# Start-up of a fused convolution and gated feed-forward kernel: decode steps, taps and softmax steps given to other engines, and another order of work

## The chip, the cores and the metric

One core of a Trainium2 chip runs the whole kernel. The metric is the device time of one execution in microseconds (us), the median of several runs. The engines are named as in the profile: PE (TensorE, with PEld for its weight loads), DVE (VectorE), ACT (ScalarE), POOL (GpSimd) and SP (the queue that issues most DMAs).

## The reference, cut to what matters

There are 4 sequences of 4160 tokens with 192 channels. Each token has its own 7 convolution weights for each of 8 heads, which go through a softmax; the result goes through a gated feed-forward part of width 1024.

```python
w = softmax(weight_gen, axis=-1)                  # per token and head, 7 taps
attn[s, h] = sum_k w[s, h, k] * x[s - 6 + k, h]   # causal, zeros ahead of the sequence
h = relu(attn @ w_in)                             # 192 -> 1024
conv = sum_k conv_w[k] * h[s - 1 + k]             # 3 taps, per channel
out = (h * sigmoid(conv)) @ w_out                 # 1024 -> 192
```

## The kernel before, in words

**Blocks.** The 16640 tokens are cut into 128 stretches of 130 tokens, one stretch to a partition. A block takes 4 tokens of every stretch, 512 in all; there are 33 blocks, called b0 to b32 here. The work of a block has these stages:

- *Softmax* (`sm_ops`, L222). Weights come in groups of 8 tokens (group 0: 4), so that group 1 serves b1 and b2, group 2 serves b3 and b4, and so on. The steps are max, subtract (`sub`, L242), exp, sum, add a small number, reciprocal, multiply (`norm`, L264). In the groups that hold a stretch's first 7 tokens, `zero` (L269) multiplies by a mask. `SMX` says for groups 0 to 3 on which engine (V is DVE, G is POOL) `sub` and `norm` run; `SMR` gives both to POOL from group 4 on.
- *Taps* (`tap`, L284, the instruction at L292). Seven products of shifted tokens and weights, each 128 x 768, into four pieces `px` and three pieces `py`. `PLAN` names the engine of each of the seven for b0, b1 and b2; later blocks have all seven on POOL.
- *Sum of the taps and transpose* (`head`, L654). In b0 to b2 (form "a") PE transposes all seven pieces and adds them up in PSUM (L327). Later blocks (form "d") add them by two accumulating DMAs issued on POOL (L315, L318) and one POOL addition (L322), and PE transposes one piece.
- *Split* (L338 on ACT, L343 on DVE) of the transposed block into a high and a low part, which PE multiplies with high and low parts of `w_in`.
- *Units* (`unit`, L708): for each of 8 slices f of the 1024 channels, five matmuls into a bank of the PSUM pool z (L359, five banks), relu (L365, ACT), the middle tap of the 3-tap convolution (L369, ACT), the two side taps (L376, DVE), tanh (L383, ACT), the gate product (L392, DVE). A z bank is free after its gate product.
- *Out tiles* (`out_tiles`, L733): 16 matmul instructions for each 128 tokens (L405), evacuation (L414, ACT), store.

**Weight decode at the start.** `w_in` comes in five pieces (`CH`; "m" rows 0 to 127, "f" the other 64 rows folded, which a DMA spreads to their place, L614), `w_out` in four (`WOE`), and `conv_w` in one. Each arrives in 64-bit floats that are decoded by integer and float steps (`dec`, L529): two on ACT (L133, L136), then clamp (L140), shift (L143), sign (L146) and add (L151). `w_in` pieces are then split into high (L595, ACT) and low (L600). The last letter of a piece's string is its mode. In mode S the bits stay in SBUF, and the first two letters name the engines of clamp and add. In mode P they are in the one bank of the PSUM pool `ps_d`, and all steps, the low part too, run on DVE whatever the letters say:

```python
mode = eng[2]
ce, je = "VV" if mode == "P" else eng[:2]
```

Pieces in mode P follow each other through `dbank`, since they share the bank; odd out tiles use it later.

**Order of the work.** All stages are tasks with an engine, an estimated duration and dependencies. A planner (L776 to L863) places them by earliest start and rank `now`, then from the end back and once more forward, keeps the shorter plan, and the instructions are issued in that order, so each engine runs a fixed list. The rank of a block's taps is its number plus `TO`, of its transposes plus `FO`, of its out tiles plus `WO_`; `FORD` is the order of the slices in b0. The engine "VK" marks a DVE task with operands in SBUF alone; the plan reserves POOL during such a task. Where a POOL task follows VK tasks in the list, L874 and L875 put a DVE memset and a POOL memset of the same small tile `tok` ahead of it, so that POOL waits until DVE has come that far:

```python
if eng[i] == "VK":
    pend = True
elif eng[i] == "G" and pend:
    t_ = tok[nk % len(tok)]
    V.memset(t_, 0.0)
    G.memset(t_, 1.0)
```

Of the kernel before, what the change touches and what calls it, by code (L numbers as in the profile page):

```python
# [17 lines left out]
TAPS = 7  # L18
# [1 line left out]
GRP = 24  # L20
G7 = "G" * 7
PLAN = (
    ("a", "GVVGGGG"),
    ("a", "GVVGGGG"),
    ("a", "GVVGGGG"),
)
REST = ("d", G7)
SMX = ("VV", "VV", "VV", "VG")
SMR = "GG"
TO = -3.05  # L30
FO = -0.65
WO_ = 1.47
NX = 3
NY = 2
NZ = 5
# [2 lines left out]
RING = 24  # L38
CG = 2
CH = (  # L40
    ("f", 0, 256, 5.2, "VVS", "V"),
    ("m", 0, 256, 8.7, "VVS", "G"),
    ("f", 256, 512, 17.0, "GGP", "G"),
    ("m", 256, 512, 16.0, "VVS", "V"),
    ("m", 512, 1024, 18.0, "VVP", "V"),
)
FORD = (1, 3, 2, 7, 0, 6, 5, 4)
SL = ((0, 1, 2), (3, 4, 5), (1, 0, 2), (4, 3, 5), (1, 4, 5))
WOE = ("VGP", "VGP", "GVS", "GVS")


def vec(n, ps=1):

    return 0.07 + n / 960 + 0.06 * ps


def act(n, ptr=0):
    return 0.05 + n / 1200 + 0.1 * ptr


def pool(n, ins=2):
    return (0.13 + n / 437) if ins == 2 else (0.1 + n / 900)
# [3 lines left out]
def kernel(  # L66
# [15 lines left out]
    HK = HEADS * TAPS  # L82
# [104 lines left out]
    def grows(j):  # L187
        return (R * (2 * j - 1), 2 * R) if j else (0, R)
# [33 lines left out]
    def sm_ops(j):  # L222
        s0, n = grows(j)
        V = nc.vector
        es = SMX[j] if j < len(SMX) else SMR
        E_ = [V if e == "V" else nc.gpsimd for e in es]
        N = n * HEADS * TAPS
        ed = [vec(N, 0) if e == "V" else pool(N) for e in es]
        ek = ["VK" if e == "V" else "G" for e in es]

        def w():
            return w_t[j][:, :n * HEADS]

        def m(k):
            return sm_t[j][k][:, :n * HEADS]

        def vmax():
            sm_t[j] = [sm_p.tile([P, 2 * R * HEADS, 1], F32, tag=t, name=t) for t in ("m", "r")]
            V.tensor_reduce(out=m(0)[:, :, 0], in_=w(), axis=AX.X, op=ALU.max)

        def sub():
            E_[0].tensor_tensor(out=w(), in0=w(), in1=m(0).to_broadcast([P, n * HEADS, TAPS]), op=ALU.subtract)  # L242

        def exp():
            nc.scalar.activation(out=w(), in_=w(), func=ACTF.Exp)

        def vsum():
            V.tensor_reduce(out=m(0)[:, :, 0], in_=w(), axis=AX.X, op=ALU.add)

        def eps():  # L250
            if j:
                nc.scalar.activation(out=m(0), in_=m(0), func=ACTF.Copy, bias=1e-9)
            else:
                V.tensor_scalar(out=m(0), in0=m(0), scalar1=1e-9, scalar2=None, op0=ALU.add)

        def rec():
            V.reciprocal(out=m(1), in_=m(0))

        def keep():
            r = m(1)[:, (n - 1) * HEADS:, :]  # L260
            V.tensor_scalar(out=r, in0=r, scalar1=mask[:, 1:2], scalar2=None, op0=ALU.mult)

        def norm():
            E_[1].tensor_tensor(out=w(), in0=w(), in1=m(1).to_broadcast([P, n * HEADS, TAPS]), op=ALU.mult)  # L264

        def zero():
            k = min(n, TAPS - s0)
            t4 = w()[:, :k * HEADS, :].rearrange("p (s h) k -> p s h k", h=HEADS)
            V.tensor_tensor(  # L269
                out=t4, in0=t4, in1=edge[:, s0:s0 + k, :].unsqueeze(2).to_broadcast([P, k, HEADS, TAPS]), op=ALU.mult  # L270
            )

        return (
            [("V", vec(N, 0), vmax), (ek[0], ed[0], sub), ("A", act(N) + 0.04, exp), ("V", vec(N, 0), vsum),
             ("A" if j else "VK", 0.16 if j else 0.1, eps), ("V", 0.07 + 0.05 * n, rec)]
            + ([("VK", 0.1, keep)] if j == NG - 1 else [])
            + [(ek[1], ed[1], norm)]
            + ([("VK", vec(N, 0), zero)] if s0 < TAPS else [])
        )

    def tap_cut(q, k):
# [140 lines left out]
    V, G = nc.vector, nc.gpsimd  # L422

    with tc.manual_schedule():
# [41 lines left out]
        def load_out(c):  # L466
            nc.sync.dma_start(
                out=r_out[c].rearrange("p (c d) b -> p c (d b)", c=2),
                in_=w_out.bitcast(I32)[2 * c * P:2 * (c + 1) * P, :].rearrange("(c p) e -> p c e", p=P),
            )  # L470
# [16 lines left out]
        def task(eng, dur, deps, fn=None, after=(), begun=()):  # L487
            edges = [(d, dur_of(d) + lat(d, eng)) for d in deps if d is not None]
            edges += [(d, dur_of(d)) for d in after if d is not None]
            edges += [(d, 0.0) for d in begun if d is not None]  # L490
            tasks.append((eng, dur, edges, fn))
            prio.append(now[0])
            return len(tasks) - 1
# [12 lines left out]
        def dma(occ, deps, fn):  # L506
            return task("none", 3.2, [task("H", occ, deps, fn)])
# [9 lines left out]
        def softmax(q, dep):  # L517
            t_ = dep
            for i, (e, d, fn) in enumerate(sm_ops(q)):
                t_ = task(e, d, [t_] + ([sm.get(q - 2)] if i == 0 else []), fn)  # L520
            sm[q] = t_
# [57 lines left out]
        def used(ix):  # L579
            return [k for i in ix for k in last_use[i]]  # L580

        for c, (kind, a, b, t, eng, wle) in enumerate(CH):
            n = b - a
# [43 lines left out]
        for c in range(4):  # L627
# [3 lines left out]
                wo[:, 2 * c:2 * c + 2].rearrange("p c d -> p (c d)").bitcast(I32), r_out[c],  # L631
                slots[iB][:, 0:w], slots[iC][:, 0:w], dma(1.6, spreads, lambda c=c: load_out(c)), used((iB, iC)), WOE[c],
            )
# [12 lines left out]
        def loads(q):  # L646
            if q >= RB:
                x_t_[q] = dma(1.2, all_taps[q - RB], lambda: load_x(R * q - 1, R * q + 3))
            g = group(q)
            if g >= WB and g not in sm:  # L650
                g0 = 2 * (g - WB)
                softmax(g, dma(0.7, all_taps[g0] + (all_taps[g0 - 1] if g0 else []), lambda: load_w(g)))

        def head(q):  # L654
# [24 lines left out]
            multi = len(out_) > 1  # L679
            now[0] = q + FO  # L680
            hold, prev = {}, [None, None]
# [26 lines left out]
        def unit(j, f):  # L708
            n = j * NF + f
            so = 1 if j else 0  # L710
            now[0] = j + (FORD.index(f) if j == 0 else f) / NF
            mm[n] = task(
# [20 lines left out]
        def out_tiles(j):  # L733
            d_ = 0.03 + NF * 0.326
            no = geom(j)[0]
            for i in range(no):
                now[0] = j + WO_ + i / R
                hold = {}
                z_ = j == NB - 1 and i % 2 == 0

                def fn(i=i, hold=hold, z_=z_):
                    hold[0] = mm2(j, i, ps_z.tile([P, W], F32, tag="z", name="z") if z_ else None)
                dep = [mm[NU - 1], (zl + zfree)[-NZ]] if z_ else bank[1 + i % 2]
                a_ = tiles[j, i] = task(
                    "P", d_, [rd[j * NF + f] for f in range(NF)] + wo_rdy + dep, fn,
                    after=[tiles.get((j, i - 1))])
                e_ = task("A", act(D) + 0.02, [a_] + (stored[-4:][:1] if i == 0 and len(stored) > 3 else []),
                          lambda hold=hold: evac(*hold[0]), begun=last_evac)
                last_evac[:] = [e_]
                if z_:  # L750
                    zfree.append(e_)
                else:
                    bank[1 + i % 2] = [e_]
                if j == NB - 1 and i % 2 == 1:
                    dma(0.5, [e_], lambda i=i: store(j, i - 1, i + 1))
            if j < NB - 1:
                stored.append(dma(1.2, [e_], lambda: store(j, 0, no)))

        def attention(q):
            now[0] = q + TO  # L760
            loads(q)
            head(q)
# [3 lines left out]
        for j in range(NB):  # L766
            if j >= 2:
                out_tiles(j - 2)
            for f in FORD if j == 0 else range(NF):
                unit(j, f)  # L770
# [137 lines left out]
```

## Time and profile before

| | us |
|---|---|
| median of 3 runs (lowest to highest) | 724.79 (724.45 to 724.89) |
| profiled execution, its own time | 722.55 |
| its span, first to last instruction | 720.8 |
| PE busy | 693.8 (96%) |
| DVE busy | 633.2 (88%) |
| ACT busy | 546.9 (76%) |
| POOL busy | 503.8 (70%) |
| mean granted TensorE clock | 0.998 |

Busy shares are averages over the span; the start has other limits than the rest, so it is read by stretches of time. A row of the timeline gives the start, the busy time, the engine, the line, the operation and, in brackets, how long the engine sat idle before it and what released it.

### The profile page before, as it was taken

What the parts mean: (1) busy time and instruction counts of PE and PEld (TensorE: products, weight loads), DVE (VectorE), ACT (ScalarE), POOL (GpSimd) and SP (SyncE); (2) the same over time, 40 slices, a digit from 0 to 9 for tenths busy, and PEclk for the clock granted to TensorE, in tenths of its full rate; (3) what the DMA queues carried; (4) which work ended last, traced back from release to release, by engine and by line L of the source; (5) the groups of instructions that cost most, each with busy time, mean ns of one, the idle gap of its engine ahead of it and who ended that gap; (6) DMA issues with size and microseconds to landing.
All of it is one profiled execution on the core that took longest, in us unless ns stands there. A gap on an engine that the chain in (4) does not pass through costs nothing.

```text
span 720.8 us, 10895 instructions
## 1 busy us (share of the span) xinstructions
PE 693.8 (96%) x3809; PEld 630.0 (87%) x3809; DVE 633.2 (88%) x981; ACT 546.9 (76%) x1049; POOL 503.8 (70%) x390
## 2 busy tenths in 40 slices
PE   2799999899999999999999999999999999999998
PEld 1678898799999999999999999999999999999998
DVE  6999997899998989989898988999888888888882
ACT  3397887787878778878787787778777777787872
POOL 3588998969888789888777687887767767810000
PEclk9999999999999999999999999999999999999999
DMA  7635999997999888888898788878887886862111
GB/s 230 174 111 119 215 216 228 208 238 167 222 204 211 195 196 190 180 194 199 199 209 196 177 188 178 197 185 202 201 189 185 187 191 133 175 150 77 69 48 45
DMA packets 70787, 127.59 MB, mean 177 GB/s; under 512 B 5046, under 2 KB 42573, under 8 KB 70732
## 3 DMA queue, kind: packets, MB, share of 16 engines
q0 software_dynamic: 20160, 58.99, 47.0%
q1 hardware_dynamic: 50090, 67.51, 28.3%
q8 instruction: 30, 0.49, 0.3%
q10 hardware_dynamic: 482, 0.40, 0.2%
q14 instruction: 25, 0.20, 0.1%
HBM read 20.51 MB, written 12.78 MB: 46 GB/s over the span
## 4 chain that ended last, share of the span: by engine, by line
PE 82%; POOL 10%; DMA 4%; issue 2%; DVE 1%; ACT 1%; SPq 0%; POOLq 0%
PE ops L405 41%; PE z L359 36%; POOL py L292 4%; POOL px L292 4%; PE tp L327 3%; DMA px<-py 2%; DMA ring<-in_x_dram 1%; POOL px L318 1%; PE z L405 1%; DMA stage<-in_moe_w_in_dram 1%; POOL px L322 0%; POOL px L315 0%; DVE px L292 0%; POOL w L242 0%; SPq L437 0%
## 5 line engine op out<-in xcount | busy, mean ns | idle before, releaser
L376 DVE SCALAR_TENSOR_TENSOR z<-h,cw,z 128x512 f32<-128x512 f32 (+1 forms) x528 | 377.6, 741 | 14.7 <-ACT z L369 10.5
L405 PE MATMUL ops<-wo,g 128*128 128x192 f32 x2048 | 353.2, 326 | 0.0
L405 PEld LDWEIGHTS ops<-wo,g 128*128 128x128 f32 x2048 | 338.8, 190 | 10.2 <-DVE H L343 0.4
L359 PE MATMUL z<-H,wi 128*128 128x512 f32 x1056 | 304.3, 410 | 3.4 <-DVE g L392 3.4
L292 POOL TENSOR_TENSOR px<-ring,w 128x768 f32<-128x768 f32 (+2 forms) x141 | 229.6, 1774 | 66.8 <-PE tp L327 66.5
L359 PEld LDWEIGHTS z<-H,wi 128*128 128x128 f32 x1056 | 191.9, 189 | 35.6 <-DVE g L392 4.4
L392 DVE SCALAR_TENSOR_TENSOR g<-z,h 128x512 f32<-128x512 f32 (+1 forms) x264 | 179.5, 681 | 34.7 <-ACT z L383 32.0
L383 ACT ACTIVATE z<-z 128x512 f32<-128x512 f32 (+1 forms) x264 | 152.1, 577 | 61.7 <-DVE z L376 60.6
L369 ACT ACTIVATE z<-h,cw 128x512 f32<-128x512 f32 (+1 forms) x264 | 180.1, 683 | 5.4
L365 ACT ACTIVATE h<-z 128x512 f32<-128x512 f32 x264 | 156.0, 592 | 34.1 <-PE z L359 33.7
L292 POOL TENSOR_TENSOR py<-ring,w 128x768 f32<-128x768 f32 (+2 forms) x109 | 167.8, 1852 | 0.0
L359 PE MATMUL z<-L,wi 128*128 128x512 f32 x264 | 103.4, 392 | 0.0
L322 POOL TENSOR_TENSOR px<-px 128x768 f32<-128x768 f32 x30 | 68.2, 2275 | 8.5 <-DMA px<-px 8.5
L318 POOL DMA_DIRECT2D px<-px x30 | 38.3, 1275 | 31.5 <-DMA px<-py 31.2
L359 PEld LDWEIGHTS z<-L,wi 128*128 128x128 f32 x264 | 49.7, 188 | 11.4
L338 ACT ACTIVATE H<-tp 128x512 fp32r<-128x512 f32 (+1 forms) x63 | 37.2, 591 | 25.5 <-PE tp L327 25.3
L327 PE MATMUL tp<-ident,px 128*128 128x128 f32 (+1 forms) x288 | 45.5, 282 | 6.6 <-POOL px L292 3.5
L414 ACT ACTIVATE o<-ops 128x192 f32<-128x192 f32 x128 | 41.8, 326 | 10.6 <-PE ops L405 10.4
L327 PEld LDWEIGHTS tp<-ident,px 128*128 128x128 f32 (+1 forms) x288 | 34.4, 133 | 15.0 <-POOL px L292 5.5
L315 POOL DMA_DIRECT2D px<-py x30 | 42.7, 1424 | 6.4 <-POOL py L292 6.3
L343 DVE TENSOR_TENSOR L<-tp,H 128x512 fp32r<-128x512 f32 x33 | 22.7, 688 | 13.5 <-ACT H L338 13.4
L343 DVE TENSOR_TENSOR H<-tp,H 64x512 fp32r<-64x512 f32 x30 | 20.5, 683 | 2.2 <-ACT H L338 1.3
(81 smaller groups left out, 187.0 us busy)
## 6 DMA issues: line engine op xcount, KB each, us to landing
px<-py POOLq DMA_DIRECT2D x30, 1152.0 KB, 10.5
h<-h SPq DMA_DIRECT2D x128, 256.0 KB, 4.9
px<-px POOLq DMA_DIRECT2D x30, 768.0 KB, 6.8
ring<-in_x_dram SPq DMA_DIRECT2D x31, 384.0 KB, 7.9
out_dram<-o SPq DMA_DIRECT2D x31, 384.0 KB, 6.9
w<-in_weight_gen_dram SPq DMA_DIRECT2D x15, 224.0 KB, 7.2
r_out<-in_moe_w_out_dram SPq DMA_DIRECT2D x4, 384.0 KB, 5.3
wi<-scr SPq DMA_DIRECT2D x8, 128.0 KB, 5.8
```

The costliest lines, as they stand in the source:

```text
L292: eng.tensor_tensor(out=dst[:, a:b, :].rearrange("p s (h g) -> p s h g", g=GRP), in0=ring[:, p:p + n, :].rearrange("p s (h g) -> p s h g", ...
L318: nc.gpsimd.dma_start(out=fl4(px_t[q][:, 0:2]), in_=fl4(px_t[q][:, 2:4]), accum_op=ALU.add, max_dma_last_dim=3072)
L322: nc.gpsimd.tensor_tensor(out=a, in0=a, in1=b, op=ALU.add)
L327: nc.tensor.matmul(dst[0:D2 if part else P, c * P:(c + 1) * P], lhsT=src[:, c, part * P:part * D2 + P], rhs=ident, is_transpose=True, star ...
L343: nc.vector.tensor_tensor(out=H[D2:P, :] if part else h_t[q, "L1"], in0=tp[r, :], in1=H[r, :].bitcast(F32), op=ALU.subtract)
L359: nc.tensor.matmul(out=z, lhsT=w[:, fs], rhs=h_t[j, nm], start=(i == 0), stop=(i == len(terms) - 1))
L365: nc.scalar.activation(out=hrow(f, 2, R), in_=z_t[j, f], func=ACTF.Relu)
L369: nc.scalar.activation(out=z_t[j, f][:, :no * P], in_=hrow(f, cc, no), func=ACTF.Copy, scale=cw[:, NF + f:NF + f + 1])
L376: nc.vector.scalar_tensor_tensor(out=z, in0=hrow(f, cc + d, no), scalar=cw[:, k * NF + f:k * NF + f + 1], in1=z, op0=ALU.mult, op1=ALU.add,)
L383: nc.scalar.activation(out=z, in_=z, func=ACTF.Tanh, scale=0.5)
L392: nc.vector.scalar_tensor_tensor(out=g_of(j, f), in0=z_t[j, f][:, :no * P], scalar=1.0, in1=hrow(f, cc, no), op0=ALU.add, op1=ALU.mult)
L405: nc.tensor.matmul(out=ps[:, 0:D], lhsT=g_of(j, f)[:, i * P:(i + 1) * P], rhs=wo[:, f, :], start=(f == 0), stop=(f == NF - 1),)
```

## The change

It gives new values to tables and to one engine argument. Taps of b1 and b2 run on POOL, all seven; in b0 the two DVE taps are numbers 1 and 4 in place of 1 and 2. `sub` and `norm` of groups 2 and 3 run on POOL. Every piece of `w_in` and `w_out` is decoded in mode P. `zero` runs on the engine of `norm` and is planned with its true size. `FORD`, `TO`, `FO` and `WO_` have new values.

```diff
 PLAN = (
-    ("a", "GVVGGGG"),
-    ("a", "GVVGGGG"),
-    ("a", "GVVGGGG"),
+    ("a", "GVGGVGG"),
+    ("a", "GGGGGGG"),
+    ("a", "GGGGGGG"),
 )
-SMX = ("VV", "VV", "VV", "VG")
+SMX = ("VV", "VV", "GG", "GG")
-TO = -3.05
-FO = -0.65
-WO_ = 1.47
+TO = -2.7
+FO = -0.35
+WO_ = 1.62
 CH = (
-    ("f", 0, 256, 5.2, "VVS", "V"),
-    ("m", 0, 256, 8.7, "VVS", "G"),
-    ("f", 256, 512, 17.0, "GGP", "G"),
-    ("m", 256, 512, 16.0, "VVS", "V"),
+    ("f", 0, 256, 5.2, "VGP", "G"),
+    ("m", 0, 256, 8.7, "VVP", "G"),
+    ("f", 256, 512, 17.0, "GVP", "V"),
+    ("m", 256, 512, 16.0, "VVP", "G"),
     ("m", 512, 1024, 18.0, "VVP", "V"),
 )
-FORD = (1, 3, 2, 7, 0, 6, 5, 4)
+FORD = (0, 3, 1, 5, 2, 4, 7, 6)
-WOE = ("VGP", "VGP", "GVS", "GVS")
+WOE = ("VVP", "VVP", "GVP", "VGP")
...
         def zero():
...
-            V.tensor_tensor(
+            E_[1].tensor_tensor(
...
-            + ([("VK", vec(N, 0), zero)] if s0 < TAPS else [])
+            + ([(ek[1], vec(min(n, TAPS - s0) * HK, 0) if ek[1] == "VK" else pool(min(n, TAPS - s0) * HK), zero)] if s0 < TAPS else [])
```

## Rows read from the trace of the kernel before

**Rows 1.** Busy time by stretch (PE, PEld, DVE, ACT, POOL; clock; DMA)
```profile
12.74:30.40 17.66, 11.33 (x61) 9.15 (x62) 16.43 (x30) 5.51 (x15) 11.47 (x13) 0.97 0.63 160
...
42.00:60.00 18.00, 16.44 (x96) 13.70 (x95) 17.30 (x37) 16.15 (x34) 12.85 (x11) 1.00 0.27 80
60.00:80.00 20.00, 19.99 (x108) 17.58 (x107) 19.61 (x31) 15.88 (x29) 19.68 (x19) 1.00 0.78 170
```
**Rows 2.** Chain that ended last, 0 to 140 us, shares by line
```profile
by line: POOL py L292 20.1%; POOL px L292 19.8%; issue 11.0%; DMA px<-py 9.6%; DMA ring<-in_x_dram 5.5%; PE z L359 5.2%; POOL px L318 4.0%; DMA stage<-in_moe_w_in_dram 3.1%; POOL px L322 2.5%; POOL px L315 2.3%; DVE px L292 2.2%; PE ops L40
```
**Rows 3.** Timeline of PE: first unit, and two late gaps
```profile
30.40 2.05 PE L359 MATMUL z<-H,wi 128*128 128x512 f32 x4
...
85.10 0.66 PE L327 MATMUL tp<-ident,px 128*128 128x128 f32 x4 [0.52 <-POOL px L322]
...
132.25 1.21 PE L359 MATMUL z<-H,wi 128*128 128x512 f32 x4 [2.25 <-DVE g L392]
```
**Rows 4.** POOL's waits for DVE: total, times, longest; then timeline
```profile
POOL tok L875 <- DVE tok L874: 24.8, 7, 9.6
...
12.68 0.10 POOL L875 MEMSET tok<- 128x1 f32 x1 [9.62 <-DVE tok L874]
...
16.93 0.10 POOL L875 MEMSET tok<- 128x1 f32 x1 [1.43 <-DVE tok L874]
...
20.79 0.10 POOL L875 MEMSET tok<- 128x1 f32 x1 [2.25 <-DVE tok L874]
```
**Rows 5.** Timeline of DVE: taps, and softmax subtract and normalise
```profile
17.64 1.71 DVE L292 TENSOR_TENSOR px<-ring,w 128x768 f32<-128x768 f32 x1
...
23.86 1.90 DVE L242 TENSOR_TENSOR w<-w,m 128x448 f32<-128x448 f32 x2
...
30.26 0.63 DVE L264 TENSOR_TENSOR w<-w,r 128x448 f32<-128x448 f32 x1
...
31.14 0.95 DVE L292 TENSOR_TENSOR px<-ring,w 128x768 f32<-128x768 f32 x1
...
54.69 1.82 DVE L292 TENSOR_TENSOR px<-ring,w 128x768 f32<-128x768 f32 x2
```
**Rows 6.** Groups of DVE by shape, 12.5 to 60 us: decode steps
```profile
L140 DVE TENSOR_SCALAR dps<-dps 128x384 f32<-128x384 f32 x2 | 1.1, 560 | 0.1
...
L143 DVE TENSOR_SCALAR scr<-wo 128x384 int32<-128x384 int32 x2 | 0.6, 350 | 0.0
...
L140 DVE TENSOR_SCALAR dps<-dps 128x256 f32<-128x256 f32 x1 | 0.4, 419 | 0.0
...
L600 DVE TENSOR_TENSOR scr<-dps,scr 128x256 fp32r<-128x256 f32 x1 | 0.4, 413 | 0.0
...
L140 DVE TENSOR_SCALAR scr<-scr 128x256 f32<-128x256 f32 x1 | 0.3, 280 | 0.0
```
**Rows 7.** Groups of POOL by shape, 12.5 to 60 us
```profile
L292 POOL TENSOR_TENSOR py<-ring,w 128x768 f32<-128x768 f32 x10 | 15.3, 1545 | 0.0
...
L600 POOL TENSOR_TENSOR wi<-scr,wi 128x256 fp32r<-128x256 f32 x1 | 1.1, 1108 | 0.0
L140 POOL TENSOR_SCALAR wo<-wo 128x384 f32<-128x384 f32 x2 | 1.0, 504 | 0.0
L264 POOL TENSOR_TENSOR w<-w,r 128x448 f32<-128x448 f32 x1 | 1.0, 968 | 0.0
```
**Rows 8.** Timeline: first and last steps of pieces in the decode bank
```profile
17.70 0.38 ACT L133 ACTIVATE dps<-stage 128x256 f32<-128x256 f32 x1
...
25.69 0.41 DVE L600 TENSOR_TENSOR scr<-dps,scr 128x256 fp32r<-128x256 f32 x1
...
45.53 0.51 ACT L133 ACTIVATE dps<-r_out 128x384 f32<-128x384 f32 x1
...
48.53 0.55 DVE L151 CUSTOM_DVE_ANT_0 wo<-dps,scr 128x768 uint16<-128x768 uint16 x1
...
56.43 0.55 DVE L151 CUSTOM_DVE_ANT_0 wo<-wo,scr 128x768 uint16<-128x768 uint16 x1
```

## The prediction

> **What bounds the kernel now.** The page gives PE 96% of the span, so only the rest can be won. The table by stretches says where it lies: from 60 us on PE is busy for 19.99 of 20 us, while DVE is already near its limit there (19.61). Before that PE is the engine that waits: 11.33 busy of 17.66 us between 12.74 and 30.40, 16.44 of 18.00 between 42 and 60. In the same two stretches DVE is busy for 16.43 and 17.30 us, so DVE is what is full at the start [rows 1]. The chain of waits up to 140 us names POOL first: its taps (L292) hold 40% [rows 2]. Yet POOL is busy for only 11.47 and 12.85 us of those stretches [rows 1]. The list of waits resolves this: POOL sits idle for 24.8 us in 7 waits for the token that DVE sets. The first, 9.62 us, ends at 12.68 and covers the arrival of data; 15.2 us are left [rows 4]. So POOL is late because it queues behind a full DVE, and PE is late because of both. Two late gaps of PE, 0.52 us at 85.10 and 2.25 us at 132.25 [rows 3], come from the same backlog: the first waits for POOL's sum directly, the second for a gate product. Everything after is dense PE work that the change leaves alone. A microsecond of earlier start of the dense stretch is a microsecond of time.
>
> **The change part by part.**
>
> *DVE loses work.* Two taps of b1 and two of b2: 0.95 each for b1's (the second is as long as the row at 31.14), 1.82 for b2's pair, 3.72 in all. Subtract of groups 2 and 3: 1.90. One normalise: 0.63 (the other was on POOL) [rows 5]. Together 6.25 us.
>
> *DVE gains work.* A clamp of 256 in the PSUM bank takes 0.42 us, in SBUF 0.28, and I take the shift as the same pair; three pieces of 256 go from mode S to P (the second "f" piece and the piece of 512 were in P before): 3 x 2 x 0.14 = 0.84. The low part of the second piece comes from POOL: 0.41. Two clamps of `w_out` come from POOL: 2 x 0.56. Their shifts go from 0.35 to about 0.56: 2 x 0.21 = 0.42 [rows 6]. Sign and add, which have two tensor operands, I leave at their lengths; the low part, also of two operands, is at 0.41 with one of them in PSUM [rows 6]. Together 2.8 us. Net, DVE is relieved of 6.25 - 2.8 = 3.45 us, all of it ahead of 57 us, where it is full; none is hidden.
>
> *DVE and POOL in each other's way.* The tap at 17.64, beside a POOL tap, took 1.71 us, the one at 31.14, with POOL idle, 0.95 [rows 5]. The work left on DVE that can meet this is b0's two taps and group 1's softmax, as before. I count no gain here; at best the 0.76 of one such tap, at worst the same lost.
>
> *POOL.* It gains four taps at 1.545 (6.2 us), two subtracts and one normalise at 0.97 (2.9), and loses the low part (1.11) and two clamps (1.01): net +7.0 us [rows 7]. No DMA moves with them, but the DMAs that POOL issues for b3 stand behind them in its list. Against that stand its waits. With the decode in PSUM and groups 2 and 3 on POOL, no "VK" task is left on DVE after group 1's softmax and b0's taps, both done near 20 us. So the first two waits after the start (1.43 and 2.25) stay, and the four later ones, 24.8 - 9.62 - 1.43 - 2.25 = 11.5 us, go [rows 4]. Net POOL reaches the taps of b3 4.5 us earlier. What is late next on POOL is then its own work, not DVE.
>
> *The decode bank.* Now seven pieces follow each other through one bank from about 17.7 us on. The two ends of a hold are 8.4 us (ACT at 17.70 to DVE's low part, 25.69 + 0.41) and 3.55 us (45.53 to 48.53 + 0.55) [rows 8]. Seven holds are 25 to 59 us. The long one was long because DVE was full of other work inside it; with less of that I take 5 us, 35 in all, and the last `w_out` piece is decoded near 53, against 56.43 + 0.55 = 56.98 before [rows 8]. The list behind it on DVE is b1's gate products; on SP the loads of `w_out` stand behind the spread of the second "f" piece, which leaves earlier if anything.
>
> *Numbers without a price.* `zero` stays on DVE, since groups 0 and 1 keep "VV"; only its planned length shrinks. The letters ahead of P do nothing. `FORD` starts b0 with the slice whose pieces come first, and the ranks only sort ties of a plan that is then redone; the cover is that PE has b1's transposes to fill with. If that cover is gone, the price is of the size of a gap seen late, 2.25 us [rows 3], either way.
>
> **The sum.** The dense stretch starts earlier by the smaller of two reliefs, DVE's 3.45 and POOL's 4.5: -3.45 us. Of the two late gaps (2.77 together) [rows 3] both depend on POOL's lag; POOL gains about one microsecond on PE, so I take half: -1.4. That is -4.9 us: the profiled execution would go from 722.55 (span 720.8) to 717.7. The median of the runs lies 2.24 above that execution, so it goes from 724.79 to **719.9 us**.
>
> **Rivals.**
>
> *A larger gain.* The 1.25 us between DVE's and POOL's relief, both late gaps and a slowed tap come on top: 4.5 + 2.77 + 0.76 = 8.0, and if the first unit at 30.40 also gains the 2 us that b0's taps lose to tokens and the low part, about 10: 715 to 717. For it: PE is idle for 6 of the 17.66 us ahead of the first unit [rows 1]. Against: DVE must take part in all of it, and is full. Chance 0.13.
>
> *The bank decides (slower).* If a hold takes 7 us on the mean, the last piece is ready at 17.7 + 49 = 66.7, 9.7 later than before. b1's gate products wait, its five z banks stay full and PE stops. With DVE's relief of 3.45 spent inside, that is +6.2: 731. It decides above (56.98 - 17.7)/7 = 5.6 us a hold. For it: one hold was 8.4. Against: that piece waited for DVE, not the bank. Chance 0.07.
>
> *POOL becomes the bound (slower).* If the waits for DVE stay, because a DVE task in SBUF is still put among b1's taps, POOL carries 7.0 us more, and b3's sum, which PE already waits for at 85.10 [rows 3], comes that much later: 731.8. It decides when more than 8.2 of the 15.2 us of waits stay [rows 4]. For it: a tap takes 1.545 on POOL against 0.95 on DVE [rows 5, 7]. Against: no such DVE task is left for b1 to b3. Chance 0.10.
> The Trainium skill (GPSIMD Engine Reference, Engine selection) speaks for this rival: it gives elementwise work of two inputs to VectorE, as GpSimd is about two times slower. By its measured ratio of 1.96 a tap would be an estimated 1.86 us on POOL, and the four moved ones 7.4 us in place of 6.2. The trace differs: its ratio is 1.6 [rows 5, 7].
>
> *Nothing moves.* The gain at the start is given back in a new gap of PE or ACT, for instance where ACT, in order, waits for a subtract that now runs on POOL: two gaps like that at 132.25 cost 4.5 us [rows 3] and leave 724.4. Chance 0.12.
>
> **Chances and range.** The forecast, with -2 to -7, has 0.58. A difference of 0.2%, 1.45 us, is about what the measurement tells from none. Faster: 0.58 + 0.13 and a little of the unpriced order = 0.72; same 0.11; slower 0.17. The range goes from 715.0 (the larger gain at most in full) to 725.5 (the gain given back and a little more); it leaves out the two slower rivals and the extreme of the larger gain.
>
> **What would show it.** Right: the waits of POOL for the token after 21 us are gone; the four DVE taps after 30 us are gone; the first unit begins before 29 us; the last decode of `w_out` ends before 55 us; b3's first accumulating DMA is issued some 4 us earlier; PE is dense from about 52 to 56 us on. Wrong: a hold of the bank above 5.6 us, a PE gap at b3's transpose longer than 0.52 us, ACT waiting for POOL's subtract before 60 us, or new gaps in PE after 60 us that add up to more than the old 2.77.

## The result and the profile after

The kernel after takes **714.72 us** (median of 4 runs, 713.11 to 715.78), the kernel before beside it 724.84 (724.45 to 725.26): a ratio of 0.9858 (95% interval 0.9839 to 0.9878), 10.1 us less. The sign was right and the size twice the forecast, just outside the range. The profiled execution took 713.11, its span is 711.4 (before 720.8). Executions of one kernel differ with their mean granted clock (the kernel before has a median near 722.9 over its recorded executions at 0.998 and near 724.8 over those at 0.991), and both traces are of the faster kind, 0.998 before and 1.000 after, so spans are compared with spans here and medians with medians.

**Where the time went.** Busy time by hundreds of microseconds (columns as in [rows 1]), the kernel before:

```profile
0.00:100.00 100.00, 78.44 (x437) 67.56 (x437) 89.34 (x173) 65.66 (x134) 73.77 (x73) 0.98 0.67 171
100.00:200.00 100.00, 97.68 (x535) 88.62 (x534) 89.52 (x137) 78.40 (x151) 87.60 (x67) 1.00 0.95 216
200.00:300.00 100.00, 100.00 (x550) 91.39 (x548) 91.39 (x139) 80.61 (x155) 84.03 (x62) 1.00 0.86 196
```

and the kernel after, with the stretches of [rows 1] behind them:

```profile
0.00:100.00 100.00, 81.89 (x471) 72.21 (x472) 91.06 (x176) 70.01 (x144) 82.53 (x75) 1.00 0.74 190
100.00:200.00 100.00, 100.00 (x550) 91.40 (x549) 92.19 (x141) 81.30 (x157) 93.63 (x71) 1.00 0.95 216
200.00:300.00 100.00, 100.00 (x549) 91.31 (x548) 91.17 (x138) 80.42 (x155) 81.59 (x60) 1.00 0.83 190
...
12.74:30.40 17.66, 12.31 (x69) 10.29 (x70) 16.08 (x33) 6.35 (x16) 13.80 (x14) 1.00 0.73 201
...
42.00:60.00 18.00, 17.99 (x108) 15.11 (x108) 17.91 (x35) 15.99 (x32) 17.68 (x14) 1.00 0.28 75
60.00:80.00 20.00, 20.00 (x110) 18.34 (x109) 19.61 (x31) 16.87 (x33) 17.51 (x17) 1.00 0.97 213
```

A dense stretch runs some 550 matmuls in 100 us. After, PE does 34 more in the first hundred (6.2 us at that rate) and 15 more in the second; 49 at 5.5 a us are 8.9 us, nearly all of the span's 9.4. From 200 us on the kernels are alike within a few matmuls in 100 us. The first hundred gains more PE work (6.2 us) than busy time (81.89 - 78.44 = 3.45): before, part of it ran at a granted clock of 0.50, the 1.2 GHz level, from 29.60 to 32.60, after PE's waits for b0, which is worth some 1.5 us of that difference; after shows 1.00. Over the whole span PE idles 5.7 us less (27.0 to 21.3) and is busy 3.7 us less (693.8 to 690.1) with the same 3809 matmuls.

The timeline of PE after, around the first unit and at b3's transpose ([rows 3]):

```profile
26.81 0.66 PE L327 MATMUL tp<-ident,px 128*128 128x128 f32 x4 [1.33 <-POOL px L292]
27.22 0.71 PE L359 MATMUL z<-H,wi 128*128 128x512 f32 x2
28.93 0.71 PE L359 MATMUL z<-H,wi 128*128 128x512 f32 x2 [1.00 <-ACT wi L595]
...
77.80 0.60 PE L327 MATMUL tp<-ident,px 128*128 128x128 f32 x4
```

The first unit begins at 27.22 in place of 30.40. After 28.93 PE has no wait in the rows up to 150 us: b3's transpose comes at 77.80 without a wait (85.10 and 0.52 before), and the gap of 2.25 at 132.25 has no successor.

POOL after: its total of waits for the token over the whole span, the last of them before 140 us, b3's two accumulating DMAs, the subtract behind the first, and its last addition ([rows 4]):

```profile
POOL tok L875 <- DVE tok L874: 14.6, 6, 9.3
...
22.73 0.10 POOL L875 MEMSET tok<- 128x1 f32 x1 [0.26 <-DVE tok L874]
...
56.54 1.41 POOL L315 DMA_DIRECT2D px<-py  x1 [0.32 <-POOL py L292]
57.50 1.46 POOL L242 TENSOR_TENSOR w<-w,m 128x448 f32<-128x448 f32 x1
58.44 6.50 POOL L292 TENSOR_TENSOR px<-ring,w 128x768 f32<-128x768 f32 x4
67.14 1.69 POOL L292 TENSOR_TENSOR py<-ring,w 128x384 f32<-128x384 f32 x2 [2.19 <-DMA px<-py]
68.77 1.21 POOL L318 DMA_DIRECT2D px<-px  x1
...
75.32 2.22 POOL L322 TENSOR_TENSOR px<-px 128x768 f32<-128x768 f32 x1
```

From 21 to 140 us POOL waits 0.26 us for DVE in all. The first DMA of b3 leaves at 56.54 (63.48 before), the addition starts at 75.32 (82.23).

DVE after: the last decode step of `w_out`, and b1's first gate product ([rows 8]):

```profile
50.90 0.55 DVE L151 CUSTOM_DVE_ANT_0 wo<-dps,scr 128x768 uint16<-128x768 uint16 x1
...
53.67 0.68 DVE L392 SCALAR_TENSOR_TENSOR g<-z,h 128x512 f32<-128x512 f32 x1
```

The decode ends at 51.45 (56.98 before), and the gate product starts 6.5 us earlier (60.20). The chain of waits up to 140 us, by line ([rows 2]), is now PE's own work:

```profile
by line: PE z L359 38.7%; PE ops L405 29.7%; PE tp L327 7.0%; DMA ring<-in_x_dram 5.0%; PE ops L327 4.4%; DMA stage<-in_moe_w_in_dram 3.5%; DVE py L292 1.2%; POOL px L292 1.1%; POOL py L292 1.1%; issue 0.9%; SPq L437 0.8%; DVE r L257 0.8%; 
```

### The profile page after: what moved, and what is told of

Same layout as the page of the kernel before. It is cut to its first block, busy times and chain, and to the rows that moved or that the text cites. A ratio compares the mean times of both kernels' runs of the same rounds, so it can differ in the third digit from the quotient of the medians.

```text
span 711.4 us, 10938 instructions
## 1 busy us (share of the span) xinstructions
PE 690.1 (97%) x3809; PEld 629.0 (88%) x3809; DVE 625.6 (88%) x975; ACT 549.9 (77%) x1049; POOL 510.5 (72%) x392
## 4 chain that ended last, share of the span: by engine, by line
PE 96%; DMA 2%; DVE 1%; POOL 0%; SPq 0%; ACT 0%; issue 0%; POOLq 0%
PE ops L405 47%; PE z L359 43%; PE tp L327 5%; DMA ring<-in_x_dram 1%; PE ops L327 1%; PE z L405 1%; DMA stage<-in_moe_w_in_dram 1%; DVE py L292 0%; POOL px L292 0%; POOL py L292 0%; SPq L437 0%; DVE r L257 0%; DVE m L248 0%; DVE w L242 0%; DVE px L292 0%
## 5 line engine op out<-in xcount | busy, mean ns | idle before, releaser
L376 DVE SCALAR_TENSOR_TENSOR z<-h,cw,z 128x512 f32<-128x512 f32 (+1 forms) x528 | 379.3, 741 | 25.7 <-ACT z L369 21.3
L292 POOL TENSOR_TENSOR py<-ring,w 128x768 f32<-128x768 f32 (+2 forms) x108 | 162.8, 1813 | 2.2 <-DMA px<-py 2.2
L318 POOL DMA_DIRECT2D px<-px x30 | 36.3, 1211 | 13.2 <-DMA px<-py 12.0
## 6 DMA issues: line engine op xcount, KB each, us to landing
px<-py POOLq DMA_DIRECT2D x30, 1152.0 KB, 10.2
```

The costliest lines, as they stand in the source:

```text
L292: eng.tensor_tensor(out=dst[:, a:b, :].rearrange("p s (h g) -> p s h g", g=GRP), in0=ring[:, p:p + n, :].rearrange("p s (h g) -> p s h g", ...
L376: nc.vector.scalar_tensor_tensor(out=z, in0=hrow(f, cc + d, no), scalar=cw[:, k * NF + f:k * NF + f + 1], in1=z, op0=ALU.mult, op1=ALU.add,)
```

## The experiments

All results together, each with the kernel before on the same chip; the expectations state the theories as they stood when each run began:

| run | median | before | ratio [95%] |
|---|---|---|---|
| b_taps: taps alone | 722.83 | 723.95 | 0.9991 [0.9980, 1.0002] |
| b_sm: softmax alone | 724.55 | 723.95 | 1.0005 [0.9991, 1.0019] |
| b_dec: decode alone | 727.14 | 723.95 | 1.0041 [1.0028, 1.0054] |
| b_ord: order alone | 726.71 | 723.95 | 1.0036 [1.0024, 1.0048] |
| a_no_taps | 724.78 | 724.13 | 1.0006 [0.9994, 1.0019] |
| a_no_sm | 718.67 | 724.13 | 0.9932 [0.9913, 0.9952] |
| a_no_dec | 722.93 | 724.13 | 0.9985 [0.9974, 0.9996] |
| a_no_ord | 724.29 | 724.13 | 1.0004 [0.9991, 1.0017] |
| a_no_taps_free | 722.04 | 724.09 | 0.9977 [0.9967, 0.9988] |
| b_free | 748.05 | 724.09 | 1.0333 [1.0316, 1.0350] |
| a_old_offs | 723.79 | 724.09 | 0.9994 [0.9982, 1.0006] |
| a_old_ford | 713.06 | 724.09 | 0.9851 [0.9836, 0.9866] |
| a_old_offs_sum3 | 722.86 | 724.35 | 0.9981 [0.9966, 0.9995] |
| a_old_fo | 722.82 | 724.35 | 0.9984 [0.9971, 0.9998] |
| a_jit2 | 716.16 | 724.35 | 0.9886 [0.9860, 0.9912] |
| a_old_offs_sum3_sub | 721.00 | 724.72 | 0.9954 [0.9938, 0.9969] |
| a_fold1_late | 717.67 | 724.52 | 0.9910 [0.9883, 0.9937] |

### Each part alone in the kernel before

The edits are the hunks of the diff above: b_taps takes `PLAN`, b_sm `SMX` and `zero`, b_dec `CH` and `WOE`, b_ord `TO`, `FO`, `WO_` and `FORD`.

> Kernel before with the new taps alone (blocks 1 and 2 all on POOL, block 0 with DVE taps 1 and 4). Theory D (the gain is work taken from DVE and waits taken from POOL, the tables of order do little): DVE loses 3.7 us, POOL gains 6.2 and keeps most of its waits for DVE, since decode in SBUF stays: 721 to 724 us. Theory O (the tables of order carry most of the gain): within 1.5 us of 724.8.

> Kernel before with the new softmax engines alone (groups 2 and 3 on POOL). Theory D: DVE loses 2.5 us, POOL gains 2.9 and loses some waits: 721 to 724 us. Theory O: within 1.5 us of 724.8.

> Kernel before with the new decode alone (all pieces in the PSUM bank). Theory D: DVE gains 2.4 us of work, POOL loses 2.1 us of work and several waits; the two reliefs only pay together, so 723 to 727 us. Theory O: within 1.5 us of 724.8. If the decode alone gives the 10 us, both are wrong: then POOL's waits for DVE were the bound.

> Kernel before with the new TO, FO, WO_ and FORD alone. Theory D: within 1.5 us of 724.8. Theory O: 717 to 721 us, with units of block 1 between the transposes of block 2 in PE's order as in the changed kernel.

No part brings anything that the measurement can tell from nothing, and two cost 0.4%. b_taps fits theory D and b_dec just misses it; the softmax alone stays at the old time, as O had it; b_ord is slower than both forecast for it. What happens shows in PE's gaps. Timeline of PE, b_taps:

```profile
29.91 1.09 PE L327 MATMUL tp<-ident,px 128*128 128x128 f32 x4 [1.92 <-DVE L L343]
...
79.14 1.19 PE L359 MATMUL z<-H,wi 128*128 128x512 f32 x4 [0.92 <-DVE g L392]
```

The same of b_dec:

```profile
46.89 1.12 PE L327 MATMUL tp<-ident,px 128*128 128x128 f32 x4 [3.37 <-DVE px L292]
```

and of b_ord:

```profile
60.04 1.12 PE L327 MATMUL tp<-ident,px 128*128 128x128 f32 x4 [3.58 <-DVE px L292]
```

With the decode or the order changed alone, PE stands before a transpose whose DVE tap is late; with the taps moved, that gap is not there, and a split on DVE and a gate product are late instead. b_sm has nearly the gaps of the kernel before (0.89 at 52.64, 0.54 at 86.16, 2.25 at 133.29).

### Each part taken out of the change

The same hunks, undone in the kernel after.

> Changed kernel with the old taps (two DVE taps in each of blocks 0, 1 and 2). Theory D: DVE gets 3.7 us back and POOL waits for it again: 717 to 720 us. Theory O: 714 to 716.5 us.

> Changed kernel with the old softmax engines (group 2 on DVE, group 3 half). Theory D: DVE gets 2.5 us back, POOL waits again: 716 to 719 us. Theory O: 714 to 716.5 us.

> Changed kernel with the old decode modes (three pieces of w_in and two of w_out in SBUF). Theory D: POOL waits for DVE's SBUF steps among the taps of blocks 0 and 1 again, DVE has 2.4 us less: 716 to 721 us. Theory O: 714 to 716.5 us.

> Changed kernel with the old TO, FO, WO_ and FORD. Theory D: within 1.5 us of 714.7. Theory O: 719 to 724 us, with gaps of PE between 42 and 60 us again.

Each loss is large: without the taps, the decode or the order, 8 to 10 us of the 10.1 are gone, without the softmax steps 4.0 (718.67 against 714.72). Summed, the four losses are 32 us, three times the gain, so the parts don't add up: leaving out any one of three of them gives most of the gain back. Theory D holds for a_no_sm alone, and the other three lose more than it forecast; theory O gave the loss to the order, and the taps and the decode lose about as much. Timeline and stretch of PE in a_no_taps:

```profile
46.55 1.11 PE L327 MATMUL tp<-ident,px 128*128 128x128 f32 x4 [4.80 <-DVE px L292]
...
46.00:52.00 6.00, 5.45 (x26) 5.02 (x27) 5.66 (x13) 1.37 (x3) 3.52 (x5) 0.50 0.24 66
```

DVE's two taps of b1 stand behind decode steps and gate products in a list without a pause, and PE waits 4.80 us for them. Then the granted clock is 0.50 for 6 us: the four transposes of the first row take 1.11 us, against 0.60 for the four at 77.80 in the kernel after. So this gap costs more than its length. In a_no_dec it is gate products that are late (1.43 at 66.48, 1.61 at 78.95), in a_no_sm as well (1.23 at 60.52, 1.15 at 63.09). But these gaps are not all: both ran at half clock around their first unit, where the kernel after shows 1.00, a_no_dec at 0.50 from 25 to 35 us and a_no_sm from 27 to 33. Stretches of a_no_dec:

```profile
12.74:30.40 17.66, 10.69 (x57) 8.11 (x57) 14.51 (x28) 5.61 (x15) 13.26 (x14) 0.84 0.61 158
30.40:42.00 11.60, 10.46 (x58) 8.97 (x59) 7.41 (x18) 5.64 (x12) 8.79 (x10) 0.80 0.60 201
```

PE is busy for 7.81 of the ten us from 25 to 35, so at half clock an estimated 3.9 us are lost there, more than in the two gaps. In a_no_ord it is b3's sum on POOL that is late:

```profile
89.06 1.12 PE L327 MATMUL tp<-ident,px 128*128 128x128 f32 x4 [4.15 <-POOL px L322]
```

### Is it the reservation of POOL that makes DVE's taps dear?

a_no_taps_free is a_no_taps with all six DVE taps planned without holding POOL:

```diff
-                p_ = task("VK" if e == "V" else e, d_, ...
+                p_ = task(e, d_, ...
```

> Changed kernel with the old taps, as a_no_taps (724.8 us), but the DVE taps are planned on DVE alone: POOL is not reserved for them and no token follows them. Theory R (a DVE tap comes late because the plan needs DVE and POOL free at once for it; PE waits 4.80 us for such a tap at 46.55 us): the gap is gone, 714 to 718 us. Rival F (DVE is simply full, so a tap on it is late however it is planned): a gap of PE behind a DVE tap stays, 721 to 726 us.

b_free is the kernel before without any reservation or token, the first edit in the planner and the second where the tokens are issued:

```diff
-        held = {"VK": ("V", "G")}
+        held = {"VK": ("V",)}
...
-            if eng[i] == "VK":
+            if False:
```

> Kernel before with no reservation of POOL for DVE's SBUF tasks and no tokens, work on the same engines. Theory R: POOL's 15.2 us of waits for DVE after the start were what held b0 to b3 back: 716 to 720 us. Rival F: DVE is full and is now slowed by POOL as well: 723 to 728 us.

Theory R fails in both. Most of the loss stays in a_no_taps_free, so the reservation alone is not what the taps cost. DVE and PE there:

```profile
29.30 1.75 DVE L292 TENSOR_TENSOR px<-ring,w 128x768 f32<-128x768 f32 x1
...
31.30 1.96 DVE L292 TENSOR_TENSOR px<-ring,w 128x768 f32<-128x768 f32 x1
...
33.52 0.67 DVE L343 TENSOR_TENSOR L<-tp,H 128x512 fp32r<-128x512 f32 x1
...
34.34 1.09 PE L327 MATMUL tp<-ident,px 128*128 128x128 f32 x4 [6.68 <-DVE L L343]
```

b1's and b2's taps take 1.65 to 1.96 us beside POOL's (0.95 alone [rows 5]), and the split that PE needs stands behind them. b_free is 20 us above rival F's range too. PE's longest wait there, then a group of DVE by shape, 12 to 140 us, and one instruction of it with POOL beside it in the timeline:

```profile
45.04 2.79 PE L327 MATMUL tp<-ident,px 128*128 128x128 f32 x12 [19.45 <-DVE L L343]
...
L143 DVE TENSOR_SCALAR scr<-wo 128x384 int32<-128x384 int32 x2 | 7.6, 3824 | 0.0
...
64.66 6.17 DVE L143 TENSOR_SCALAR scr<-wo 128x384 int32<-128x384 int32 x1
...
64.09 6.51 POOL L292 TENSOR_TENSOR px<-ring,w 128x768 f32<-128x768 f32 x4
```

The largest part of the loss is the wait of 19.45 us. The split that ends it stands behind DVE's steps on SBUF, which are slow beside POOL's taps: between 21 and 44 us a clamp takes 1.63 us (0.28 in [rows 6]), a low part 1.76 (0.42 at 33.80 in the kernel before), three taps 1.69 to 2.29 (0.95 alone). The shift shows how far this can go: 350 ns in the kernel before [rows 6], 3824 on the mean here. The one at 64.66 lasts 6.17 us: it begins inside a run of four POOL taps, which ends at 70.60, and ends 0.23 us behind it; the other lasts 1.48. So a DVE step on SBUF can be held up for a whole run of POOL's taps and not only for one. POOL's 15 us of waits buy DVE's speed; they are saved by taking SBUF work off DVE, as the change does, and not by dropping the token.

### Which of the new order's values carries its part?

a_old_offs is the kernel after with the old `TO`, `FO` and `WO_`, a_old_ford with the old `FORD`, a_old_fo with `FO = -0.65` alone, a_jit2 with all three ranks a step further:

```diff
-TO = -2.7
-FO = -0.35
-WO_ = 1.62
+TO = -2.65
+FO = -0.3
+WO_ = 1.65
```

> Changed kernel with the old TO, FO and WO_, new FORD. Theory R says nothing of order; a_no_ord lost all of the gain (724.3 us) with a gap of 4.15 us at 89.06 us behind the sum of block 3 on POOL. If the offsets place that sum: 721 to 725 us and the gap is there. If it was FORD: 714 to 717 us.

> Changed kernel with the old FORD, new offsets. If the offsets carry the part of the order: 714 to 717 us and no gap at 89 us. If FORD carries it: 721 to 725 us.

> Changed kernel with the old FO alone (the rank of the transposes); its list for POOL has the second accumulating DMA of block 3 behind the last taps of block 5, as with all old offsets. Theory L: a gap of 4 to 5 us near 89 us, 721 to 725 us. Rival (TO or WO_ carries it): 713 to 717 us.

> Changed kernel with TO -2.65, FO -0.3, WO_ 1.65 in place of -2.7, -0.35, 1.62: a small shift in the same direction; in POOL's list the sum of block 3 stands as early as in the changed kernel. Theory L: 713 to 717 us. If the gain hangs on these exact values: 718 us or more.

`FORD` is worth nothing that shows: with the old one the time is that of the kernel after, within the intervals. `FO` alone is worth 8 of the 10 us, as theory L forecast. Timeline of POOL, then PE, in a_old_fo:

```profile
25.16 1.89 POOL L242 TENSOR_TENSOR w<-w,m 128x448 f32<-128x448 f32 x2
27.01 3.04 POOL L292 TENSOR_TENSOR px<-ring,w 128x768 f32<-128x768 f32 x2
30.01 0.98 POOL L264 TENSOR_TENSOR w<-w,r 128x448 f32<-128x448 f32 x1
31.21 0.97 POOL L264 TENSOR_TENSOR w<-w,r 128x448 f32<-128x448 f32 x1 [0.23 <-DVE r L257]
...
59.17 1.54 POOL L292 TENSOR_TENSOR px<-ring,w 128x768 f32<-128x768 f32 x1
60.66 1.29 POOL L315 DMA_DIRECT2D px<-py  x1
...
69.79 4.83 POOL L292 TENSOR_TENSOR py<-ring,w 128x384 f32<-128x384 f32 x5 [3.26 <-DMA px<-py]
...
76.20 1.17 POOL L318 DMA_DIRECT2D px<-px  x1
...
85.54 2.72 POOL L322 TENSOR_TENSOR px<-px 128x768 f32<-128x768 f32 x1
...
88.31 1.11 PE L327 MATMUL tp<-ident,px 128*128 128x128 f32 x4 [4.68 <-POOL px L322]
```

With the old rank, group 3's subtract and normalise, which b5 needs, stand at b1's first taps and ahead of all others of b1 and b2, and one more tap stands ahead of b3's first accumulating DMA. That DMA leaves 4.1 us later than after (60.66 against 56.54), POOL sits 3.26 us for its landing in place of 2.19, more tap pieces stand ahead of the second DMA (five `py` and two `px` pieces in place of two `py`; 7.4 later), and b3's addition comes 10.2 us later. PE waits 4.68 us, and from 85 to 95 us its clock is 0.66 on the mean. The median of a_jit2 is 1.4 us above that of the change, within the intervals; its trace, of the slowest of its five executions (719.54), has small gaps at other places.

### Does moving b3's sum alone repair the old ranks?

a_old_offs_sum3 moves b3's second accumulating DMA three tap-sized POOL tasks and its addition five tasks ahead in a_old_offs; a_old_offs_sum3_sub also moves group 4's subtract (and the max ahead of it) by four:

```diff
+        for i, back_ in zip(sum3, (3, 5)):
+            k = issue.index(i)
+            g = [n for n in range(k) if eng[issue[n]] == "G" and tasks[issue[n]][3] is not None][-back_]
+            issue.insert(g, issue.pop(k))
```

> a_old_offs (723.8 us) with two entries of POOL's list moved and nothing else: the second accumulating DMA of block 3 is issued three tap tasks earlier (before POOL's last pieces of block 5 instead of behind them), and the last addition of block 3 five tasks earlier. Theory L (the offsets matter through this place in POOL's list: PE waits 4.63 us at 89.5 us for that addition, and its clock is halved for some 8 us behind the wait): the addition ends near 80 us, the gap and the low clock are gone, 714 to 717.5 us. Rival O (the old offsets order PE, DVE and ACT badly as a whole): the gap goes but others open, 719 to 724 us.

> a_old_offs_sum3 (722.9 us) with one more move: the subtract of group 4 on POOL and the maximum on DVE that it needs go four POOL tasks earlier, ahead of two taps, an accumulating DMA and another tap. In a_old_offs_sum3 ACT stood still for 6.25 us up to 94.0 us with the exp of that group at the head of its list, and PE lost 4.30 us at 99.77 us. Theory L (the old offsets lose at such single places of POOL's list that others wait for in order): ACT's wait falls below 2 us, PE's gap at 99.8 us is gone, 714 to 718 us. Rival O (the order as a whole): another gap opens and it stays at 720 to 724 us.

Theory L fails in both: the places that were moved are in time, yet the time stays in rival O's range. The gap moves and does not go. (In a_old_offs the clock is 0.50 from 90 to 95 us and 0.98 from 95 to 100, so it is low for some 6 us behind the wait, not 8.) In a_old_offs_sum3 ACT, then PE:

```profile
94.03 0.58 ACT L245 ACTIVATE w<-w 128x448 f32<-128x448 f32 x1 [6.25 <-POOL w L242]
...
99.77 1.73 PE L359 MATMUL z<-H,wi 128*128 128x512 f32 x4 [4.30 <-DVE g L392]
```

With the subtract earlier too, it is b4's sum that is late:

```profile
107.87 0.76 PE L327 MATMUL tp<-ident,px 128*128 128x128 f32 x4 [4.49 <-POOL px L322]
```

POOL issues the first DMAs of b3 and b4 at 60.13 and 76.98 there, 3.6 and 3.5 us later than after; the moves change who waits for that lag, not the lag.

### One DMA later, and nothing else

a_fold1_late is the kernel after with b3's first accumulating DMA issued behind the subtract and the first two of the taps that follow it:

```diff
+        k = issue.index(first3[0])
+        g = [n for n in range(k + 1, nt) if eng[issue[n]] == "G" and tasks[issue[n]][3] is not None][2]
+        issue.insert(g, issue.pop(k))
```

> Changed kernel with one entry of POOL's list moved: the first accumulating DMA of block 3 is issued behind the softmax subtract and two taps that follow it, 3.9 us later (near 60.5 us, where it stands with the old offsets). Theory S (the old offsets lose because POOL issues that DMA 3.6 to 4.7 us late, behind work that is not urgent, and everything of b3 and b4 on POOL follows by that much, with no slack left on PE): b3's last addition ends 3 to 4 us later, PE waits 2.5 to 3.5 us for it near 78 us, 717 to 720.5 us. Rival O (the order of all engines): POOL waits 2.19 us for that DMA anyway and takes the rest from its own slack, no gap over 1 us: 714 to 716.5 us.

```profile
60.57 1.21 POOL L315 DMA_DIRECT2D px<-py  x1
...
69.90 1.69 POOL L292 TENSOR_TENSOR py<-ring,w 128x384 f32<-128x384 f32 x2 [5.03 <-DMA px<-py]
...
78.05 2.24 POOL L322 TENSOR_TENSOR px<-px 128x768 f32<-128x768 f32 x1
...
80.34 0.66 PE L327 MATMUL tp<-ident,px 128*128 128x128 f32 x4 [1.85 <-POOL px L322]
...
80.00:85.00 5.00, 4.66 (x18) 4.33 (x19) 3.43 (x6) 2.95 (x5) 5.00 (x8) 0.66 1.04 183
```

The rows are POOL's and PE's timeline and a stretch of PE in this kernel. The DMA leaves 4.0 us later with no work added (0.5 us of this is a later start of POOL's whole list in this execution, 12.77 against 12.31), POOL's wait for its landing grows from 2.19 to 5.03, the addition comes 2.7 us later, PE has its first gap after 30 us, 1.85, and the five us from 80 on run at a mean clock of 0.66. Theory S holds, with a shorter gap than it forecast. The medians differ by 3.0 us (717.67 against 714.72, and the intervals of the two ratios don't meet); the spans of the two traces differ by 4.3 (715.6 and 711.4), of which the gap is 1.85, the five us at 0.66 about 1.7 and the later start 0.5. So the place of one issue instruction in POOL's list carries some 3 us by itself; the rest of `FO`'s 8 was not tried apart, group 3's steps ahead of the taps and the later second DMA being the candidates.

## Why the prediction was right in sign and half in size

**What held.** DVE full at the start and POOL late through its tokens were read rightly: POOL's waits for tokens after 21 us are gone but for 0.26, the four DVE taps are gone, the first unit comes before 29, the last decode ends before 55. Seven holds of the decode bank are 17.97 to 51.45 without the pauses between them, 4.8 us on the mean (5 taken). One hold was 5.9, above my mark of 5.6, without harm, since the mean decides. "POOL becomes the bound" did not come either: its waits for the token did not stay.

**The reliefs were too small.** 3.45 and 4.5 us were forecast. b1's first gate product comes 6.5 us earlier; the sum step and reciprocal of group 3 and one convolution, some 1.8 us, are done ahead of it only before, so DVE's real relief at that point is near 4.7. Part of the difference is the shift in SBUF: I took 0.28 for it, but one before took 1.03 (at 21.50), and in the bank it takes 0.42. That DVE and POOL would gain nothing from being less in each other's way came out so on balance: group 1's subtract takes 1.02 in place of 1.75 and one tap of b0 0.94 in place of 1.48, but the add step of `conv_w` 1.18 in place of 0.27 and `zero` 0.67 in place of 0.32. b3's first DMA leaves 6.9 us earlier, not 4.5. I had put 2.9 us of softmax ahead of it; in the trace after, one subtract (24.28) and one normalise (28.21) stand there, where one normalise stood before, so only 0.97 was added, and the other subtract and normalise follow it (57.50 and 74.30). That is 1.9 of the 2.4.

**The step that failed.** "The dense stretch starts earlier by the smaller of two reliefs" treats the start as one block that is shifted, and "I take half" of the late gaps then keeps part of the backlog. The runs show something else. The first matmul of a block's units comes 3.2 us earlier than before in b0, only 2.5 in b1 (45.45 against 47.90), then 5.5 in b2, 6.2 in b3, 9.1 in b4 and 9.5 in b32: the gain is made step by step up to 115 us. There are several feeders (DVE taps, splits, gate products behind the decode, POOL's sums), each with its own time at which PE needs it. If one is late, PE has a gap there, often with a slow stretch; if all are in time, every gap goes. After the first unit of the kernel before, PE's gaps were 4.74 us (0.41, 1.19, 0.37 and the two of [rows 3]); the three us at half clock lie in and just ahead of that unit. All of that went. In the terms of the sum: the end of the first unit comes 2.96 us earlier (29.71 in place of 32.67) and the three gaps before 56 us are worth 1.97, so the start is worth 4.9 where 3.45 stood; the late gaps are worth their full 2.77 where 1.4 stood; and 1.7 stood nowhere, PE's busy time for the same 3744 matmuls from there to the end (680.2 and 678.5), which I can't place. Together this is the 9.4 us of the spans. My larger-gain rival counted the late gaps in full, but I gave it 0.13, because "DVE must take part in all of it, and is full"; DVE stayed full and was in time.

**"Numbers without a price".** I put `FORD`, `TO`, `FO` and `WO_` together as ranks that "only sort ties" with a gap of 2.25 us as price. For `FORD` that held. For `FO` it was the worst sentence of the text: it is 8 us. It decides whether steps of later groups and taps of the next block stand ahead of a DMA of some 10 us (10.2 in the page after) in POOL's list; 3 of the 8 us are shown to hang on that. The trace before had the row for it: px<-py DMAs hold 9.6% of the chain [rows 2], and I passed it by.

**What stays open.** Why exactly the decode alone and the order alone cost 3 us is read from their gaps, not isolated. How the 8 us of `FO` divide is open beyond the 3 us above. No run separates the waits of PE from the low clock that comes with them. In b_taps, b_sm, b_ord, a_no_sm and a_no_dec PE ran 7 to 10 us at 0.50 around its first unit, so part of what these runs lose may be the clock alone.

## What to carry to other kernels

When the engine that bounds the kernel has several feeders, a change that relieves one of them alone may show nothing, and parts that are worth nothing alone may be worth 1.4% together; so price a change by the list of what the bound engine waits for, each with its slack, and test parts by taking them out as well as by adding them. In a list that an engine runs in order, the issue of a DMA with a long landing goes ahead of all work that isn't due: work behind it covers the landing, work ahead of it delays it. A tuning number that sorts a plan is not free of a price because it adds no instruction.

## What the runs showed of the hardware

Two things I had not expected. A DVE shift on SBUF of 350 ns took 6.17 us beside four POOL taps in a row; the slowed DVE tap that I knew took 1.71. And some PE gaps came with stretches in which the granted clock was at its 1.2 GHz level, 0.50 over 6 us in a_no_taps (gap of 4.80) and 0.66 on the mean over 5 us in a_fold1_late (gap of 1.85), whereas the kernel after shows 1.00 from its first unit to 700 us. The length of the gap does not settle it: the 2.25 us at 132.25 in the kernel before left the clock at 1.00, and a_old_ford, whose two waits at the first unit are those of the kernel after (1.34 and 0.99 in place of 1.33 and 1.00), ran at 0.50 from 30 to 32 us.
